# Two attentions over one x on one core: the first projection cut to 512 tokens, x's tiles loaded and turned in another order, the last products on the whole array

## The chip, the core and the metric

The kernel runs on one core of a Trainium2 chip. TensorE (PE) multiplies matrices into PSUM, VectorE (DVE) and ScalarE (ACT) read PSUM and work elementwise, GpSimd (POOL) works on SBUF only, and DMAs are issued from the queues of SP (SyncE), ScalarE and GpSimd. The metric is the device time of one execution in microseconds (us), the lower the better.

## The reference, cut to what matters

B = 1, S = 2048 tokens, D = 512, H = 32 heads of 16. Attention A has one k and v for all heads, attention B has its own per head. A gate mixes the two.

```python
x = A_x
g = sigmoid((x * gate_w).sum(-1, keepdims=True))
# A: q = x @ wq (32 heads), k = x @ wk and v = x @ wv (one head of 16)
# B: q, k, v = x @ wqkv, 32 heads each
# each: softmax(q k^T * 16 ** -0.5) v, heads joined, then @ wo
a = A(x, A_wq, A_wk, A_wv, A_wo)
b = B(x, B_wqkv, B_wo)
return g * a + (1 - g) * b
```

## The kernel before

**Numbers.** Every operand of a projection is split into two f16 parts, hi and lo (x by `x_split`, weights by `split_weight` on GpSimd, results by `split` on VectorE), and a product is three partial products, listed in `PARTS`. `by_tiles` (L189) does one partial product of 128x512 as eight matmuls of 64 rows and 32 columns of the array. The row halves go into two banks, which VectorE adds afterwards (`added`, L193 and L194, or the two adds of L450).

**Head.** The 16 tiles of x (128 tokens each, 256 KB) are loaded into `acc` by SP (L212). Each is turned by four transposes (`x_turn`, L264) and split: hi by ScalarE (L268), lo by VectorE (L269), into `xT`. `x_pair` does two tiles in one PSUM tile `pt`, `x_one` one tile in one bank of `aux`. Before the first exp the program turns tiles 0 to 7, projects the first 1024 tokens to the queries of A's first eight heads (192 matmuls in two units of 96), makes k and v of tiles 0 to 3 (`kv_products`, L297, 48 matmuls) and turns k (`k_turned`, L318, into `kA`), then turns tiles 8 to 11. Queries are laid out for the scores by 32 small DMAs (`lay`, L338): four tiles Q of two heads each (p = 0 to 3), each by eight pieces. The table `first` deals the pieces over the queues of SP, ScalarE and GpSimd.

**Exps.** The work is 2048 blocks u of two banks of 128 keys x 512 queries. Per block: `scores(u)` (L529, eight matmuls into one of two PSUM tiles `sc`), one exp on ScalarE (L533, 128x1024, into `pr`), and half a unit of `values` (L548, 16 matmuls, or eight pairs over two banks, two or more blocks later). One group is eight heads of A or B, in order a, b, a, b, ...: 256 blocks. Blocks 0 to 31 are p = 0 and 1 with the first 512 queries, 32 to 63 p = 2 and 3, and from block 64 on the second 512 queries are used. Block u uses key tile (u // 2) % 16, so k of tiles 4 to 7 is used from block 8 on, of 8 to 11 from 16, of 12 to 15 from 24.

**What lies between.** Each loop turn issues the scores, then what the table `early` has for this block, then values, then projection steps of eight matmuls, as many as a planner, `_Tasks`, thinks fit beside an exp (`EXP = 916`, `SCORES = 213`, `HALF = 428`, `PRODUCT = 216`, ns). Units have a block from which they may start and one at which they are due. `late()` adds up what is due; if it says so, an odd block gets one step more than fits. A unit of 12 steps starts only if its two banks (the pair of `aux` that the values don't use) stay free for it, that is not close before the pair changes, each 32 blocks. `add_side` queues work for VectorE, `move` queues `lay` calls, one per six blocks. Engines run their instructions in this program order.

**Tail.** After the last values, `emptied` adds the two banks (`raw`), DMAs sums and denominators apart (`oT`, `dT`), and `norm_pieces` gives per tile of 128 tokens `over` (reciprocal, L462) and `parts` (scaling L469, hi by ScalarE L470 and lo by GpSimd L471 for the last four tiles). `o_unit` multiplies with wo (three partial products, 24 matmuls), adds both banks into `acc` (L450, twice) and stores the tile (L452). What is left when the blocks are done is issued by `flush`.

## Time and profile before

| | us |
|---|---|
| median of 3 runs | 1957.51 |
| lowest, highest | 1956.01, 1959.62 |
| the profiled execution | 1959.14 |
| its span, first to last instruction | 1956.9 |
| ScalarE busy in the span | 1895.2 (97%) |
| TensorE busy | 1857.9 (95%) |
| VectorE busy | 756.9 (39%) |
| GpSimd busy | 444.7 (23%) |

The span is what the trace shows; the execution's time has 2.2 us more around it. A busy TensorE is not TensorE at its peak, since its matmuls overlap. The mean granted clock of TensorE over the span is 0.991 of full speed.

### The profile page before, as it was taken

The page shows a single profiled execution, that of the slowest core. Times are in us where ns is not written, and L with a number is a line of the kernel's source. Part 1 is how long each engine was busy: PE and PEld are TensorE (multiplying, and loading weights), DVE is VectorE, ACT ScalarE, POOL GpSimd, SP SyncE. Part 2 cuts the span into 40 slices and gives each one's busy share as a digit, 9 for nine tenths or more (in the row PEclk, how much of TensorE's full clock was granted, in tenths as well). Part 3 has the DMA queues.
Part 4 walks back from the last instruction along what each step waited for, and adds up shares of the span by engine and source line. Part 5 has one row for each costly group of instructions (what it writes and reads, how often), then busy time and mean ns, then how long its engine had stood idle before and what let it go on. Part 6 is the DMA issues. An engine that isn't in the chain of part 4 may idle for free.

```text
span 1956.9 us, 127404 instructions
## 1 busy us (share of the span) xinstructions
PE 1857.9 (95%) x59664; PEld 1060.7 (54%) x59664; DVE 756.9 (39%) x1429; ACT 1895.2 (97%) x2071; POOL 444.7 (23%) x840
## 2 busy tenths in 40 slices
PE   7999999999999999999999999999999999999995
PEld 4555655454555655555455655555455555555442
DVE  5344434343233344424234334443324334443432
ACT  4999999999999999999999999999999999999994
POOL 5344033230054031223034203302303502030000
PEclk8999999999999999999999999999999999999997
DMA  4121011110022010111012101100101201011101
GB/s 143 25 55 36 10 37 34 33 34 15 11 55 49 12 34 19 29 36 33 13 35 42 39 15 31 37 21 25 36 14 32 58 15 25 21 36 31 36 25 42
DMA packets 55736, 65.01 MB, mean 33 GB/s; under 512 B 21440, under 2 KB 29632, under 8 KB 55200
## 3 DMA queue, kind: packets, MB, share of 16 engines
q0 software_dynamic: 24112, 24.89, 6.4%
q1 hardware_dynamic: 30400, 31.46, 6.2%
q8 instruction: 469, 7.68, 1.7%
q14 instruction: 67, 0.55, 0.1%
q10 hardware_dynamic: 688, 0.43, 0.1%
HBM read 10.55 MB, written 4.19 MB: 8 GB/s over the span
## 4 chain that ended last, share of the span: by engine, by line
ACT 83%; issue 8%; PE 7%; DVE 2%; DMA 0%; SPq 0%; POOL 0%; ACTq 0%; DVEq 0%
ACT pr L533 82%; PE aux L548 3%; PE sc L529 2%; PE aux L189 2%; DVE xT L269 0%; DVE acc L450 0%; DMA acc<-in_A_x_dram 0%; PE aux L416 0%; ACT xT L268 0%; DVE dTb L462 0%; PE pt L264 0%; PE aux L297 0%; DMA dTb<-rawb 0%; PE aux L318 0%; PE aux L264 0%
## 5 line engine op out<-in xcount | busy, mean ns | idle before, releaser
L533 ACT ACTIVATE pr<-sc 128x1024 f32<-128x1024 f32 x2048 | 1884.6, 1191 | 12.6 <-PE sc L529 11.7
L548 PE MATMUL aux<-pr,vA 64*32 64x256 f32 x16384 | 685.3, 377 | 2.3 <-issue 1.9
L548 PE MATMUL aux<-pr,vB 64*32 64x256 f32 x16384 | 646.7, 376 | 0.1
L529 PE MATMUL sc<-Qa,kA 64*32 64x512 f16 x8192 | 453.4, 384 | 18.4 <-issue 0.3
L529 PE MATMUL sc<-Qb,K 64*32 64x512 f16 x8192 | 424.1, 385 | 41.8
L529 PEld LDWEIGHTS <-K 64*32 64x32 f16 x8192 | 209.3, 89 | 387.5 <-issue 309.0
L548 PEld LDWEIGHTS aux<-pr,vA 64*32 64x32 f32 x16384 | 335.7, 105 | 58.0 <-issue 15.1
L529 PEld LDWEIGHTS <-kA 64*32 64x32 f16 x8192 | 209.7, 90 | 277.3 <-issue 207.3
L548 PEld LDWEIGHTS aux<-pr,vB 64*32 64x32 f32 x16384 | 309.7, 105 | 35.4 <-issue 0.7
L450 DVE SCALAR_TENSOR_TENSOR acc<-aux,gate_up,acc 128x512 f32<-128x512 f32 x240 | 180.2, 751 | 326.6 <-PE aux L189 312.9
L338 POOL DMA_DIRECT2D Qa<-hia x118 | 57.8, 489 | 449.4 <-PE sc L529 299.1
L338 POOL DMA_DIRECT2D Qb<-hib x128 | 62.3, 486 | 359.5 <-DVE hib L201 181.7
L189 PE MATMUL aux<-w16ob,o16b 64*32 64x512 f16 x1536 | 80.3, 391 | 15.1 <-ACT o16b L470 13.2
L189 PE MATMUL aux<-xT,w16vb 64*32 64x512 f16 x1536 | 93.8, 376 | 0.1
L193 DVE TENSOR_SCALAR rawb<-aux 128x512 f32<-128x512 f32 x32 | 22.1, 689 | 179.9 <-PE aux L548 179.7
L338 POOL DMA_DIRECT2D K<-hik x128 | 61.5, 485 | 109.3 <-DVE hik L201 102.4
L189 PE MATMUL aux<-xT,w16kb 64*32 64x512 f16 x1536 | 82.2, 376 | 0.0
L189 PE MATMUL aux<-xT,w16qb 64*32 64x512 f16 x1536 | 79.9, 376 | 0.0
L189 PE MATMUL aux<-xT,w16qa 64*32 64x512 f16 x1536 | 79.5, 376 | 0.4 <-DVE xT L269 0.2
L189 PE MATMUL aux<-w16oa,o16a 64*32 64x512 f16 x1536 | 79.3, 376 | 0.0
L462 DVE RECIPROCAL dTa<-dTa 128x128 f32<-128x128 f32 x64 | 55.6, 918 | 59.8 <-DMA dTa<-rawa 59.8
L462 DVE RECIPROCAL dTb<-dTb 128x128 f32<-128x128 f32 x64 | 55.4, 916 | 52.9 <-DMA dTb<-rawb 52.9
(135 smaller groups left out, 991.2 us busy)
## 6 DMA issues: line engine op xcount, KB each, us to landing
acc<-in_A_x_dram SPq DMA_DIRECT2D x16, 256.0 KB, 5.9
dTa<-rawa SPq DMA_DIRECT2D x128, 32.0 KB, 2.6
oTa<-rawa SPq DMA_DIRECT2D x128, 32.0 KB, 3.2
K<-hik POOLq DMA_DIRECT2D x128, 32.0 KB, 2.7
K<-lok POOLq DMA_DIRECT2D x128, 32.0 KB, 2.9
Qb<-hib POOLq DMA_DIRECT2D x128, 32.0 KB, 2.5
Qb<-lob POOLq DMA_DIRECT2D x128, 32.0 KB, 2.8
out_dram<-acc SPq DMA_DIRECT2D x16, 256.0 KB, 2.6
```

The lines of the kernel that those rows point to most:

```text
L189: nc.tensor.matmul(out[n : n + COLS], lhsT[r, n : n + COLS], rhs[r], start=start, stop=stop)
L193: nc.vector.tensor_scalar(dst, outs[0], scale, None, op0=ALU.mult)
L338: queues[(8 * p + n) % len(queues)].dma_start(op[to : to + DH].rearrange("d (a q) -> d a q", a=2), state[part][rows])
L450: nc.vector.scalar_tensor_tensor(acc[:, t], bank, g, acc[:, t], op0=ALU.mult, op1=ALU.add)
L462: nc.vector.reciprocal(d, d)
L529: nc.tensor.matmul(sc[a : a + COLS, i], k[r, c * P + a : c * P + a + COLS], Q[src, gi, half, p][r, j * BLK : (j + 1) * BLK], start=True, s ...
L533: nc.scalar.activation(probs[u][:, :m], sc[:, :m], AF.Exp, scale=SCALE / (UP * UP))
L548: nc.tensor.matmul(o[32 * i : 32 * i + 32, cols], v[r], probs[at // ACT][r, at % ACT, cols], start=c == half == 0, stop=c == NT - 1 and ha ...
```

## The change

**Loads.** The q weights of the first group are asked for first and the o weights behind the three small loads of k, v and gate weights; x's tiles 0 to 3 stand ahead of both in the code. **Head.** Before the first exp only tiles 0 to 7 are turned, tiles 0 to 3 are projected (96 matmuls), and tiles 4 to 7 are turned behind the k and v of tiles 0 to 3. The second 512 tokens are a unit for the planner (from block 24, due at 40). `lay` moves half tiles, the first half over three queues, the second half by GpSimd. **Between exps.** `early` has one function per block: pieces of k and v (12 matmuls each), turns, and x's tiles 8 to 15, whose hi part is VectorE's too. **Tail.** For the last four tiles reciprocal and scaling alternate per tile, all of them are issued before the products, and `o_last` replaces `o_unit`: three matmuls over the whole array into one bank, one add, stores from SP and ScalarE by turns.

```diff
     def flush(self):
-        ahead = 0
         while self.open or self.units or self.side:
-            if self.side and ahead < 6 and not (self.units and ahead > 2):
+            while self.side and not self.open:
                 self.side.popleft()[1]()
-                ahead += 1
-                continue
-            ahead -= 3
...
-    first_w = load_w("a", 0, (nc.scalar, nc.gpsimd))
+    for t in range(4):
+        load_x(t, nc.sync)
+    first_w = load_w("a", 0, (nc.scalar, nc.gpsimd), ("q",))
     nc.scalar.activation(warm, warm, AF.Exp)
-    for t in range(NT):
+    for t in range(4, NT):
         load_x(t, nc.sync)
...
+    first_w += load_w("a", 0, (nc.scalar, nc.gpsimd), ("o",))
...
-        nc.scalar.activation(xT[:, 0, :, at], pt, AF.Copy, scale=UP)
+        if t < 8:
+            nc.scalar.activation(xT[:, 0, :, at], pt, AF.Copy, scale=UP)
+        else:
+            nc.vector.tensor_scalar(xT[:, 0, :, at], pt, UP, None, op0=ALU.mult)
...
+                        (nc.gpsimd if i else queues[(8 * p + n) % len(queues)]).dma_start(
+                            op[to : to + DH, i * BLK : (i + 1) * BLK], state[part][rows, i])
...
-            if i:
+            if late is not None:
+                todo.move([lambda p=p: lay(p, i) for p in range(4)])
+            elif i:
                 todo.move([lambda p=p: lay(p) for p in range(4)])
...
+    def o_last(src, gi, t, o16):
+        w, i = weights[src, gi, "o"], "ab".index(src)
+        bank = aux[t // 2 % 2][t % 2]
+        for n, (a, b) in enumerate(PARTS):
+            nc.tensor.matmul(bank, o16[:, a], w[:, b], start=n == 0, stop=n == 2)
+        nc.vector.scalar_tensor_tensor(acc[:, t], bank, gate_up[:, i, t : t + 1], acc[:, t], op0=ALU.mult, op1=ALU.add)
+        (nc.sync, nc.scalar)[t % 2].dma_start(out[t * P : (t + 1) * P, :], acc[:, t])
...
+            if ends:
+                todo.add([[lambda: o_last(src, gi, 8 * half + t8, o16)]], todo.now, todo.now)
+                return
...
-    x_pair(0)
+    for t in range(4):
+        x_one(t, aux[t // 2][t % 2])
     first_w[0]()
-    x_pair(2)
-    split_weight(wkv16[:, 0], wkv16[:, 1], wkv)
+    split(wkv16[:, 0], wkv16[:, 1], wkv)
+    nc.gpsimd.tensor_scalar(wkv, wkv, UP, None, op0=ALU.mult)
     first_w[1]()
-    for t in range(4, 8):
-        x_one(t, aux[t // 2 % 2][t % 2])
     late = []
-    first = (nc.sync, nc.scalar, nc.gpsimd, nc.sync) * 2 + (nc.sync, nc.gpsimd, nc.sync) * 8
+    first = (nc.sync, nc.gpsimd, nc.scalar, nc.sync, nc.gpsimd, nc.scalar, nc.sync, nc.gpsimd)
     turn[0] = 1
-    for unit in q_units("a", 0, 0, first, late):
-        for f in unit:
-            f()
-        turn[0] ^= 1
+    q_first, q_second = q_units("a", 0, 0, first, late)
+    for f in q_first:
+        f()
     while todo.moves:
         todo.moves.popleft()()
+    todo.add([q_second], 24, 40, 2200)
     for i in range(4):
-        kv_products(0, i, aux[0][0])
-    k_turned(0, aux[0][1])
-    x_pair(8)
-    x_one(10, aux[1][0])
-    x_one(11, aux[1][1])
+        kv_products(0, i, aux[1][0])
+    for t in range(4, 6):
+        x_one(t, aux[0][t % 2])
+    k_turned(0, aux[1][1])
+    for t in range(6, 8):
+        x_one(t, aux[0][t % 2])
...
-    early = {0: p1, 2: t1, 4: x_unit(12), 6: x_unit(13), 8: x_unit(14), 10: p2, 12: t2, 14: x_unit(15), 16: p3, 20: t3}
+    early = []
+    for b in range(1, 4):
+        if b > 1:
+            early += [x_unit(t)[0] for t in range(4 * b, 4 * b + 4)]
+        early += [f for unit in kv_units(b) for f in unit]
+    early = {u: [f] for u, f in enumerate(early)}
...
-            todo.add_side(over, todo.now + (4 if last and half else 10), [950])
-            todo.add_side(parts, todo.now + (4 if last and half else 13), [800])
+            if ends:
+                todo.add_side([f for both in zip(over, parts) for f in both], todo.now + 4, [950, 800])
+                return
+            todo.add_side(over, todo.now + 10, [950])
+            todo.add_side(parts, todo.now + 13, [800])
...
-            todo.add(q_units(src, gi, 1, pool), now if n else 21, start(n, 1) - 24, 2200)
+            todo.add(q_units(src, gi, 1, pool), now if n else 24, start(n, 1) - 24, 2200)
```

In the rows below, which come from the built programs and have no time in them, a name's number is its buffer, and the line numbers of the changed program are its own.

On ScalarE's queue ahead of the first exp (`pr<-sc`), before: the split of tile 7, two pieces of Q, and the splits of tiles 8 to 11.

```order
L268 ACTIVATE xT<-aux_85 128x4x128
L338 DMA Qa_399<-loa_194 16x1024 x2
L268 ACTIVATE xT<-pt_500 128x4x128 x2
L268 ACTIVATE xT<-aux_84 128x4x128
L268 ACTIVATE xT<-aux_85 128x4x128
L533 ACTIVATE pr_550<-sc_541 128x1024
```

Now, where four more pieces of Q stand right ahead of these:

```order
L339 DMA Qa_289<-hia_167 16x512
L339 DMA Qa_289<-loa_168 16x512
L339 DMA Qa_298<-hia_167 16x512
L339 DMA Qa_298<-loa_168 16x512
L270 ACTIVATE xT<-aux_82 128x4x128
L270 ACTIVATE xT<-aux_83 128x4x128
L270 ACTIVATE xT<-aux_82 128x4x128
L270 ACTIVATE xT<-aux_83 128x4x128
L553 ACTIVATE pr_420<-sc_411 128x1024
```

Eight issues of Q's pieces now stand ahead of the splits of tiles 4 to 7, and these ahead of the first exp; tiles 8 to 11 are gone from this place.

On VectorE after the first k turn between exps (`kA`), before: lo parts of x's tiles 12 to 14 and two maxima of weights (`stats`).

```order
L319 COPY kA<-aux_83 128x512
L269 SCALAR_TENSOR_TENSOR xT<-aux_82,xT 128x4x128
L198 TENSOR_REDUCE stats<-wqa_104 128x1
L198 TENSOR_REDUCE stats<-woa_107 128x1
L269 SCALAR_TENSOR_TENSOR xT<-aux_83,xT 128x4x128
L269 SCALAR_TENSOR_TENSOR xT<-aux_82,xT 128x4x128
```

Now, at the same place:

```order
L316 COPY kA<-aux_83 128x512
L194 TENSOR_REDUCE stats<-wqa_108 128x1
L272 TENSOR_SCALAR xT<-aux_82 128x4x128
L273 SCALAR_TENSOR_TENSOR xT<-aux_82,xT 128x4x128
L194 TENSOR_REDUCE stats<-woa_127 128x1
L272 TENSOR_SCALAR xT<-aux_83 128x4x128
L273 SCALAR_TENSOR_TENSOR xT<-aux_83,xT 128x4x128
L272 TENSOR_SCALAR xT<-aux_82 128x4x128
L273 SCALAR_TENSOR_TENSOR xT<-aux_82,xT 128x4x128
L272 TENSOR_SCALAR xT<-aux_83 128x4x128
L273 SCALAR_TENSOR_TENSOR xT<-aux_83,xT 128x4x128
```

Four tiles, 8 to 11, stand there with two instructions each, where three tiles had one each.

On VectorE in the tail, behind the last `raw`, before:

```order
L462 RECIPROCAL dTb_52040<-dTb_52040 128x128 x4
L469 SCALAR_TENSOR_TENSOR oTb_52039<-oTb_52039,dTb_52040 128x128
L450 SCALAR_TENSOR_TENSOR acc<-aux_84,gate_up,acc 128x512
L450 SCALAR_TENSOR_TENSOR acc<-aux_85,gate_up,acc 128x512
L469 SCALAR_TENSOR_TENSOR oTb_52039<-oTb_52039,dTb_52040 128x128
L450 SCALAR_TENSOR_TENSOR acc<-aux_84,gate_up,acc 128x512
L450 SCALAR_TENSOR_TENSOR acc<-aux_85,gate_up,acc 128x512
L469 SCALAR_TENSOR_TENSOR oTb_52039<-oTb_52039,dTb_52040 128x128 x2
L450 SCALAR_TENSOR_TENSOR acc<-aux_84,gate_up,acc 128x512
L450 SCALAR_TENSOR_TENSOR acc<-aux_85,gate_up,acc 128x512
L450 SCALAR_TENSOR_TENSOR acc<-aux_84,gate_up,acc 128x512
L450 SCALAR_TENSOR_TENSOR acc<-aux_85,gate_up,acc 128x512
```

Now:

```order
L475 RECIPROCAL dTb_52069<-dTb_52069 128x128
L482 SCALAR_TENSOR_TENSOR oTb_52068<-oTb_52068,dTb_52069 128x128
L475 RECIPROCAL dTb_52069<-dTb_52069 128x128
L482 SCALAR_TENSOR_TENSOR oTb_52068<-oTb_52068,dTb_52069 128x128
L475 RECIPROCAL dTb_52069<-dTb_52069 128x128
L482 SCALAR_TENSOR_TENSOR oTb_52068<-oTb_52068,dTb_52069 128x128
L475 RECIPROCAL dTb_52069<-dTb_52069 128x128
L482 SCALAR_TENSOR_TENSOR oTb_52068<-oTb_52068,dTb_52069 128x128
L444 SCALAR_TENSOR_TENSOR acc<-aux_82,gate_up,acc 128x512
L444 SCALAR_TENSOR_TENSOR acc<-aux_83,gate_up,acc 128x512
L444 SCALAR_TENSOR_TENSOR acc<-aux_84,gate_up,acc 128x512
L444 SCALAR_TENSOR_TENSOR acc<-aux_85,gate_up,acc 128x512
```

Reciprocals and scalings now stand ahead of all adds, the reciprocals one per scaling, and each tile has one add from a bank of its own in place of two from a shared pair.

## Rows read from the trace of the kernel before

**Rows 1.** The page's chain that ended last: shares of the span by line.

```profile
ACT pr L533 82%; PE aux L548 3%; PE sc L529 2%; PE aux L189 2%; DVE xT L269 0%; DVE acc L450 0%; DMA acc<-in_A_x_dram 0%; PE aux L416 0%; ACT xT L268 0%; DVE dTb L462 0%; PE pt L264 0%; PE aux L297 0%; DMA dTb<-rawb 0%; PE aux L318 0%; PE aux L264 0%
```

**Rows 2.** The chain near the end: start us, length us, engine and line.

```profile
1914.03 0.87 ACT pr L533
...
1925.95 1.25 ACT pr L533
```

**Rows 3.** Timeline, head: start us, busy us, engine, line, operation, out<-in, count, idle before.

```profile
7.69 1.12 PE L264 MATMUL pt<-ident,acc 128*128 128x128 f32 x4 [0.24 <-DMA acc<-in_A_x_dram]
...
8.43 1.15 POOL L207 TENSOR_TENSOR w16qa<-wqa,w16qa 128x512 f16<-128x512 f32 x1
...
10.19 0.60 ACT L268 ACTIVATE xT<-pt 128x512 f16<-128x512 f32 x1 [0.76 <-DVE xT L269]
...
10.82 0.69 DVE L269 SCALAR_TENSOR_TENSOR xT<-pt,xT 128x512 f16<-128x512 f32 x1 [0.66 <-ACT xT L268]
...
21.82 1.42 ACTq L338 DMA_DIRECT2D Qa<-loa  x2
...
28.42 1.04 ACT L533 ACTIVATE pr<-sc 128x1024 f32<-128x1024 f32 x1
...
36.96 0.66 PE L264 MATMUL aux<-ident,acc 128*128 128x128 f32 x4
...
41.98 1.36 PE L297 MATMUL aux<-wkv,xT 128*128 128x33 f16 x48 [0.81 <-DVE xT L269]
```

**Rows 4.** Stretches: the exps alone: us, busy (count), clock, DMA share, GB/s.

```profile
28.00:60.00 32.00, 24.27 (x26) 0.94 0.18 48
```

**Rows 5.** The chain, head: start us, length us, engine, buffer and line.

```profile
12.76 2.85 PE aux L189 x95
...
18.74 0.61 DVE ya L193
...
30.68 0.13 DVE k L304
...
32.13 0.61 PE aux L318 x4
...
60.79 0.71 ACT pr L533
```

**Rows 6.** Timeline of the tail, columns as in Rows 3.

```profile
1933.13 3.39 DVE L462 RECIPROCAL dTb<-dTb 128x128 f32<-128x128 f32 x4 [3.27 <-DMA dTb<-rawb]
...
1936.43 0.23 DVE L469 SCALAR_TENSOR_TENSOR oTb<-oTb,dTb 128x128 f32<-128x128 f32 x1
...
1936.70 0.30 ACT L470 CAST o16b<-oTb 128x128 f16<-128x128 f32 x1 [9.50 <-DVE oTb L469]
...
1945.43 1.48 PE L189 MATMUL aux<-w16ob,o16b 64*32 64x512 f16 x24 [2.25 <-ACT o16b L470]
...
1946.98 1.62 DVE L450 SCALAR_TENSOR_TENSOR acc<-aux,gate_up,acc 128x512 f32<-128x512 f32 x2 [1.73 <-PE aux L189]
```

**Rows 7.** The chain's last piece on VectorE.

```profile
1951.04 0.75 DVE acc L450
```

**Rows 8.** Stretches, all engines, after the last values.

```profile
1933.20:1951.80 18.60, 6.71 (x96) 1.40 (x96) 10.07 (x16) 1.10 (x4) 1.65 (x4) 0.50 0.13 45
```

**Rows 9.** The page's DMA issues: queue, count, KB each, us to landing.

```profile
acc<-in_A_x_dram SPq DMA_DIRECT2D x16, 256.0 KB, 5.9
...
out_dram<-acc SPq DMA_DIRECT2D x16, 256.0 KB, 2.6
```

**Rows 10.** Timeline of TensorE in a stretch with doubled products.

```profile
615.46 0.63 PE L548 MATMUL aux<-pr,vA 64*32 64x256 f32 x16
...
615.89 0.63 PE L189 MATMUL aux<-xT,w16vb 64*32 64x512 f16 x16
...
617.83 0.63 PE L189 MATMUL aux<-xT,w16vb 64*32 64x512 f16 x16
```

**Rows 11.** The page's groups: one that GpSimd issues.

```profile
L338 POOL DMA_DIRECT2D Qa<-hia x118 | 57.8, 489 | 449.4 <-PE sc L529 299.1
```

More of the change, by code (lines that the diff above doesn't have):

```diff
@@ L215, in _fast, with load_w @@
     todo = _Tasks()
-    def load_w(src, gi, queues=(nc.sync, nc.sync)):
+    def load_w(src, gi, queues=(nc.sync, nc.sync), which=("q", "k", "v", "o")):
         cols = slice(gi * P, (gi + 1) * P)
@@ L222, in one @@
         def one(part, at, bufs):
+            if part not in which:
+                return
             w = inp.tile([P, BLK], F32, tag="in", name=f"w{part}{src}{gi}")
@@ L267, in x_split @@
         at = slice(t * P, (t + 1) * P)
-        nc.scalar.activation(xT[:, 0, :, at], pt, AF.Copy, scale=UP)
+        if t < 8:
+            nc.scalar.activation(xT[:, 0, :, at], pt, AF.Copy, scale=UP)
+        else:
+            nc.vector.tensor_scalar(xT[:, 0, :, at], pt, UP, None, op0=ALU.mult)
         nc.vector.scalar_tensor_tensor(xT[:, 1, :, at], pt, UP, xT[:, 0, :, at], op0=ALU.mult, op1=ALU.subtract)
-    def x_pair(t2):
-        pt = ps_s.tile([P, 2, NK, P], F32, tag="sc", name=f"pt{t2}")
-        for i in range(2):
-            x_turn(t2 + i, pt[:, i])
-        for i in range(2):
-            x_split(t2 + i, pt[:, i])
     def x_one(t, bank):
@@ L330, in project, with lay @@
         state = {}
-        def lay(p):
+        def lay(p, i=None):
             op, n = put(p), 0
@@ L337, in lay @@
                     to = hh * 64 + n % 4 * DH
-                    queues[(8 * p + n) % len(queues)].dma_start(
-                        op[to : to + DH].rearrange("d (a q) -> d a q", a=2), state[part][rows])
+                    if i is None:
+                        queues[(8 * p + n) % len(queues)].dma_start(
+                            op[to : to + DH].rearrange("d (a q) -> d a q", a=2), state[part][rows])
+                    else:
+                        (nc.gpsimd if i else queues[(8 * p + n) % len(queues)]).dma_start(
+                            op[to : to + DH, i * BLK : (i + 1) * BLK], state[part][rows, i])
                     n += 1
@@ L357, in product @@
             split(state["hi"][:, i], state["lo"][:, i], y)
-            if i:
+            if late is not None:
+                todo.move([lambda p=p: lay(p, i) for p in range(4)])
+            elif i:
                 todo.move([lambda p=p: lay(p) for p in range(4)])
-            if late is None:
+            if late is None or i:
                 absmax(kind, n0 + i, y)
@@ L375, in put @@
         def put(p):
-            Q[src, gi, half, p] = ops.tile([P, 2 * BLK], F16, tag="Q", name=f"Q{src}{gi}{half}{p}", bufs=8)
+            if (src, gi, half, p) not in Q:
+                Q[src, gi, half, p] = ops.tile([P, 2 * BLK], F16, tag="Q", name=f"Q{src}{gi}{half}{p}", bufs=8)
             return Q[src, gi, half, p]
@@ L573, in emptied @@
             over, parts = zip(*[norm_pieces(src, gi, half, t8, last) for t8 in range(4 * j, 4 * j + 4)])
-            todo.add_side(over, todo.now + (4 if last and half else 10), [950])
-            todo.add_side(parts, todo.now + (4 if last and half else 13), [800])
+            if ends:
+                todo.add_side([f for both in zip(over, parts) for f in both], todo.now + 4, [950, 800])
+                return
+            todo.add_side(over, todo.now + 10, [950])
+            todo.add_side(parts, todo.now + 13, [800])
     def flag_stats():
```

1 line of the change is left out of this document (removed).

## The prediction

> **What bounds the kernel now.** I read the page first, then the head and the tail in the timeline and the chain, then stretches. Of the chain that ends last, 82% of a span of 1956.9 us is ScalarE's exps [rows 1]. So an edit counts only if it starts the first exp sooner, spares ScalarE a gap between exps, or shortens what follows the last one. The last 14 exps begin at 1914.03 and the last of them at 1925.95 [rows 2], so the pace is 11.92/13 = 0.917. 2048 exps at that pace are 1878 us. The first starts at 28.42 [rows 3], the last ends at 1914.03 + 13.16 = 1927.2, and 29.7 us follow. These sum to 1936: some 21 us are lost between exps. The first 26 exps lose most: they begin before 60 us [rows 4], the 27th at 60.79 [rows 5], so 32.37 us went by where 26 x 0.917 = 23.8 would do, a loss of 8.5. (I count exps as blocks from 0, each with two 512-column score banks.)
>
> **The tail.** Before, VectorE runs four reciprocals from 1933.13, then per tile a scaling, and behind it two bank adds; the next tile's scaling stands behind them [rows 6], so each tile pays the whole round of VectorE, ScalarE, TensorE and VectorE again. The last add starts at 1951.04 [rows 7] and ends at 1951.8; 5.1 us of store and closing follow. In the changed order four pairs of reciprocal and scaling come first, then four adds, one per tile. Reciprocals step by (1936.43 - 1933.13)/4 = 0.825, a scaling takes 0.23: four pairs end at 1933.13 + 4 x 1.055 = 1937.35. The first tiles' products lie beside the later pairs. The fourth scaling starts at 1937.12; ScalarE's copy 0.27 later, at 1937.39 (as 1936.43 to 1936.70); 0.30 for the copy and 0.04 to hand over put its products at 1937.73, with GpSimd's subtraction beside the first two of them; and the sum is ready 1.55 later (1945.43 to 1946.98), at 1939.3 [rows 6]. Three whole-array products move the same 3 x 512 columns as 24 products of which eight share the array, so I take the same 1.55; the row holds at the clock of 0.50 that this stretch was granted [rows 8], after TensorE had idled. The first three adds of 0.75 run 1937.35 to 1939.6, the fourth ends at 1940.35. That is 11.4 us earlier. The stores went out one per round and now all go within 2.5 us: a lone store lands in 2.6 us, sixteen crowded loads of the same size in 5.9 [rows 9]. Four are nearer to the lone case: I take 0.4 off, **11.0 gained**, between 8.1 and 11.4.
>
> **The head.** On SP the first instruction is still x's tile 0 and on ScalarE still the q weights; what moves is the o weights, behind three small loads on GpSimd. Tile 3's transposes began at 7.69 [rows 3], after four x tiles and two weights of 256 KB each: with one of the six out of the way at most a sixth of those 7 us is saved, and nothing if the contest is only shifted. I take 7.3. (The Trainium skill, DMA: Bandwidth & Descriptors, Issuing engines are not separate DMA queues, says that transfers of all issuers share the same 16 DMA engines and interleave; by it x gains only from bytes that are taken away, not from its place in the code. No row here tells the two apart; with nothing saved the sum would be 0.4 less.) Then four transposes 1.12, ScalarE's split 0.60, VectorE's 0.69: 9.8 with the hand-overs. The q weights are split by 8.43 + 1.15 = 9.58, as before. Now 96 products. As many took 2.85 before (12.76 to 15.61 [rows 5]); 24 took 1.48 at a clock of 0.50 [rows 6, 8], so 96 would take up to 5.9. Tile 3's four transposes took 1.12 against 0.66 later [rows 3]: TensorE starts slow, and now only 16 transposes, with gaps, lead in. I take 4.7, ending at 14.5. VectorE's five steps, 3.13 (15.61 to 18.74 [rows 5]), give hi at 16.95 and lo at 17.65. Here the change adds a wait: eight DMA issues on ScalarE, where two took 1.42 [rows 3], stand ahead of the splits of tiles 4 to 7 and so of all exps. The second needs lo, so they end at 17.65 + 7 x 0.71 = 22.6. Then tiles 4 and 5 are split; tile 6 needs tile 4's bank back: 22.6 + 0.60 + 0.69 + 0.05 = 23.95; two tiles' transposes at 1.12, ScalarE 0.60: the first exp at 26.9, **1.5 gained**. With a fast TensorE throughout (2.85; 0.66 twice) and tile 3 at 7.0 it is 23.8, with 5.9 and 7.7 it is 28.5. The k/v weight split on VectorE lies in the idle time under those products; of the pieces of p = 0 and 1, GpSimd and SP issue six each, from 17.65 on: at 0.49 to 0.7 and with 2.6 to land [rows 9, 11] they are there by 24.5.
>
> **The first 24 blocks** now carry eight x tiles, twelve k/v pieces and three k turns. A plain block costs TensorE 0.43 for values (615.46 to 615.89). Two blocks with 24 products took 1.94 (to 617.83 from 615.89): less two values 1.08 is left for three groups of eight products and two of scores, each eight instructions that share the array: 0.216 each [rows 10]. So scores and values are 0.64. An x tile adds 0.59 (0.66 less the overlap with the next, an estimate) [rows 3]: 1.23, or 0.31 over the pace, 2.5 for eight. A k/v piece is a fourth of 1.36 [rows 3]: 0.98, 0.07 over, for nine of them with values 0.6. Each turn waits in TensorE's order for VectorE's chain from 30.68 to 32.13, 1.45, after the last piece, then takes its own 0.4 (0.61 at 32.13 [rows 5], less at speed), 0.43 for values and 0.22 for the next scores: 2.5, of which the two exps that ScalarE has in hand cover 1.83. That is 0.7 for the first turn; I estimate 0.9 for the second, when less is in hand, and 1.6 for the third, behind three weight maxima on VectorE. VectorE works 1.4 per x tile, more than a block's length, which holds the fourth tile back by another 0.9. Sum 7.2, plus 0.8 for blocks run before TensorE is fast again: 8.0 against 8.5, **0.5 gained**. Bounds: TensorE's own excess alone, 3.1; with slow products up to block 8, 11.
>
> **Crowding afterwards.** The second 512 tokens' projection and what is due behind it now wait until block 37. The planner then counts itself late and puts 16 products (two steps of eight) into odd blocks: by the order of its instructions 26 times before block 128 where it was none, and 27 against 18 times up to block 350; from there on the two orders agree until block 2004. Such a pair of blocks lasts the 1.94 of [rows 10] where two exps need 1.83: 0.11 each, 35 x 0.11 = 3.8; the first pair of a burst is partly covered by TensorE's lead of one score tile, so I take **3.3 lost** (1.5 to 6). The 32 extra DMA issues on GpSimd at 0.49 [rows 11] from block 44 on cost nothing as long as block 64 finds its pieces (the third rival prices that).
>
> **Sum.** 11.0 + 1.5 + 0.5 - 3.3 = 9.7. The profiled execution took 1959.14 us, 2.2 around its span; it would take 1949.4. The median of the three runs is 1957.51, 1.6 lower: **1947.8**.
>
> **Rivals.** *The crowding costs double*: an in-order TensorE that waits for VectorE in the first blocks (11 lost there, not 8.0) and again under the bursts (6, not 3.3). For it: VectorE's work in the first 24 blocks, eight tiles at 1.4 plus chains and maxima, fills nearly all of their 22 us. Against it: afterwards it has time. Gain 4.0: 1953.5. *TensorE fast from the first product*: the first exp at 23.8 and no slow blocks: gain 9.7 + 3.1 + 0.8 = 13.6, 1943.9. Against it: the doubled duration of the first transposes. (The Trainium skill, TensorE: Matmul & The Clock Gate, What's actually happening, has half rate as the resting state, released by activity; the 0.50 of [rows 8] after idling agrees, and by it this rival is unlikely.) *Slower*: the second half of Q arrives late for block 64. Its products end with block 44, at 26.9 + 8.0 + 44 x 0.917 = 75.2; VectorE 3.1; GpSimd then issues eight pieces for p = 0 and eight for p = 1, 16 x 0.49 = 7.8, from 78.3 to 86.1, and landing takes some 2.6 [rows 9, 11]: 89. Block 64 begins at 93.6. Only if it came 5 us later would block 64 wait, and from 15 us on the whole gain is gone. Against it: on GpSimd's queue only four weights' splits stand ahead, twelve steps like the 1.15 of [rows 3], handed to it from block 12 on. *The stores crowd as the loads did*: 3 less, 1950.7. *Nothing happens at the head*: 1.5 less, 1949.3, in the main case's range.
>
> **Chances.** As summed, 1944.5 to 1951.2: 0.66, the crowded stores with it. Crowding doubled 0.15, fast from the start 0.13, slower 0.03, others 0.03. The range from 1942.5 to 1953.5 leaves out the ends of both middle rivals. A measurement of this kernel tells 0.2%, 3.9 us, from nothing, so faster means under 1953.6: 0.66 + 0.13 + two thirds of 0.15 = 0.89; same 0.07; slower 0.04.
>
> **What would show it.** Right: the last add ends 13 us after the last exp, not 24.6; eight issues on ScalarE's queue before the first exp, which starts near 27; the 27th exp near 59; exps at 1.02 in odd blocks between 37 and 125. Wrong: a first exp after 28.5, a landing of the last store over 5 us, an exp near block 64 that waits for Q, or a stall over 2 us at a k turn.

## The result, and the profile after

The changed kernel takes 1961.15 us (median of 20 runs, 1957.41 to 1964.83), the kernel before 1956.43 (20 runs): a ratio of 1.0021 [1.0014, 1.0028], taken over all runs of both. 1947.8 was forecast. The profiled execution spans 1959.7 us where before spanned 1956.9, so 2.8 us are to be found in the two traces. The medians differ by 4.7 us: the profiled execution of before was one of its slower ones (1959.14), and the rest is in no trace.

The share of the exps in the chain fell from 82% [rows 1] to 79%, and links appear in it that were not there, GpSimd's issues of Qb and the landing of Qb. The page's chain by line:

```profile
ACT pr L553 79%; PE aux L568 3%; PE sc L549 2%; PE aux L185 1%; DMA acc<-in_A_x_dram 1%; PE aux L265 0%; POOL Qb L336 0%; PE aux L294 0%; DMA Qa<-hia 0%; PE aux L443 0%; DMA Qb<-lob 0%; DVE dTb L475 0%; DMA dTb<-rawb 0%; POOL K L336 0%; DMA K<-hik 0%
```

The ledger is made by counting exps. The view of one line's instructions gives for a window their count and the first and last start; what exceeds 0.9166 us for each step, the pace of the last exps in both traces, is lost. The loss is a net one, since plain blocks step by as little as 0.90. Of after, in four windows (at the head, to 275 us, around block 256, the rest):

```profile
L553 ACT ACTIVATE pr<-sc x31: 1018/1024/1098, 25.4 to 65.5; 128x1024 f32<-128x1024 f32 x31
```
```profile
L553 ACT ACTIVATE pr<-sc x220: 1017/1046/1243, 65.5 to 274.2; 128x1024 f32<-128x1024 f32 x110
```
```profile
L553 ACT ACTIVATE pr<-sc x35: 1018/1098/1245, 274.2 to 309.6; 128x1024 f32<-128x1024 f32 x35
```
```profile
L553 ACT ACTIVATE pr<-sc x1765: 1018/1239/1247, 309.6 to 1935.0; 128x1024 f32<-128x1024 f32 x197
```

The first says 40.1 us for 30 steps, 12.6 lost. Counted alike in both traces:

| stretch | before | after | difference | forecast |
|---|---|---|---|---|
| first exp starts at | 28.42 | 25.44 | -3.0 | -1.5 |
| lost, to 66 us | 8.6 | 12.6 | +4.0 | -0.5 |
| lost, 66 to 275 us | 4.0 | 8.0 | +4.0 | +3.3 |
| lost, 275 to 310 us | 0.1 | 4.2 | +4.2 | not priced |
| lost, 310 us to the last exp | 8.7 | 8.5 | -0.2 | 0 |
| last exp's start to the end of the span | 30.9 | 24.7 | -6.2 | -11.0 |
| sum | | | +2.8 | -9.7 |

The ledger is that of one execution of each kernel. The long stretch behind 310 us is not steady: in the changed kernel and its variants it lost from 8.5 to 16.9 us.

**Head.** The timeline, columns as in [rows 3], answers to that group:

```profile
7.64 0.66 PE L265 MATMUL aux<-ident,acc 128*128 128x128 f32 x4 [0.23 <-DMA acc<-in_A_x_dram]
...
9.63 2.57 PE L185 MATMUL aux<-xT,w16qa 64*32 64x512 f16 x88 [0.23 <-POOL w16qa L203]
...
15.24 0.60 ACTq L339 DMA_DIRECT2D Qa<-hia  x1
...
21.47 1.08 ACT L270 ACTIVATE xT<-aux 128x512 f16<-128x512 f32 x2 [12.53 <-DMA Qa<-hia]
...
22.84 1.97 PE L265 MATMUL aux<-ident,acc 128*128 128x128 f32 x8 [4.94 <-DVE xT L273]
...
25.44 1.02 ACT L553 ACTIVATE pr<-sc 128x1024 f32<-128x1024 f32 x1
```

Tile 3 is turned at 7.64 in 0.66 us, and the projection ends at 9.63 + 2.57 = 12.2. The two turns that come last took 1.97. The windows of these stretches (us, busy us and count of PE, PEld, DVE, ACT and POOL, clock, DMA share, GB/s), the tail's last with them, show the granted clock: 1.00 (2.4 GHz) at the projection, 0.50 (1.2 GHz) where TensorE had idled before.

```profile
8.99:12.20 3.21, 2.98 (x99) 1.42 (x99) 1.20 (x3) 0.00 (x0) 2.27 (x3) 1.00 1.04 394
22.80:24.90 2.10, 2.06 (x16) 1.69 (x16) 1.19 (x3) 0.65 (x2) 0.00 (x0) 0.50 0.14 31
1947.40:1953.00 5.60, 4.45 (x10) 1.34 (x10) 2.97 (x4) 0.00 (x0) 1.50 (x4) 0.50 0.33 121
```

**First blocks.** Block 4, which turns the second group's keys, with VectorE's operations on them and GpSimd's splits of the next group's weights beside them; then one block with a tile of x:

```profile
28.79 0.61 POOL L202 CAST w16kb<-wkb 128x512 f16<-128x512 f32 x1
...
29.02 0.43 DVE L304 TENSOR_SCALAR k<-k 128x64 f32<-128x64 f32 x1
...
29.48 1.20 POOL L203 TENSOR_TENSOR w16kb<-wkb,w16kb 128x512 f16<-128x512 f32 x1
29.71 1.06 DVE L198 SCALAR_TENSOR_TENSOR kn<-k,kn 128x64 f16<-128x64 f32 x1
...
31.74 0.61 PE L315 MATMUL aux<-ident,kn 128*128 128x128 f16 x4 [2.29 <-DVE kn L308]
```
```profile
48.17 1.02 ACT L553 ACTIVATE pr<-sc 128x1024 f32<-128x1024 f32 x1 [0.37 <-PE sc L549]
...
48.56 0.66 PE L568 MATMUL aux<-pr,vA 64*32 64x256 f32 x16
...
49.02 0.42 PE L549 MATMUL sc<-Qa,kA 64*32 64x512 f16 x8
...
49.37 0.66 PE L265 MATMUL aux<-ident,acc 128*128 128x128 f32 x4
...
49.56 1.02 ACT L553 ACTIVATE pr<-sc 128x1024 f32<-128x1024 f32 x1 [0.37 <-PE sc L549]
...
49.95 0.66 PE L568 MATMUL aux<-pr,vA 64*32 64x256 f32 x16
```

VectorE's two operations end at 29.45 and 30.77, 0.05 and 0.09 us behind GpSimd's. In a block with a tile TensorE goes from values (48.56) to scores (49.02), to the tile (49.37) and to the next values (49.95): 0.46, 0.35 and 0.58, in all 1.39, as the exps' starts do.

**Block 256**, the first of the second group: GpSimd issues its first query piece, and TensorE's scores wait:

```profile
274.40 0.48 POOL L336 DMA_DIRECT2D Qb<-hib  x1 [78.60 <-PE sc L549]
...
284.42 0.61 PE L549 MATMUL sc<-Qb,K 64*32 64x512 f16 x4 [2.47 <-DMA Qb<-lob]
```

Before, the same first piece:

```profile
263.61 0.56 POOL L338 DMA_DIRECT2D Qb<-hib  x1 [96.39 <-DVE hib L201]
```

Blocks 256 and 257 use sixteen pieces. The sixteenth left at 281.57 and landed at 284.29, 0.13 us ahead of the scores that waited; before, it landed at 273.52, and block 257 began its scores at 276.01.

**Tail**, answering to [rows 6] and [rows 7]:

```profile
1942.18 0.95 DVE L475 RECIPROCAL dTb<-dTb 128x128 f32<-128x128 f32 x1 [3.31 <-DMA dTb<-rawb]
...
1943.37 0.94 DVE L475 RECIPROCAL dTb<-dTb 128x128 f32<-128x128 f32 x1
1943.49 0.30 ACT L483 CAST o16b<-oTb 128x128 f16<-128x128 f32 x1 [7.29 <-DVE oTb L482]
...
1947.06 0.30 ACT L483 CAST o16b<-oTb 128x128 f16<-128x128 f32 x1 [0.89 <-DVE oTb L482]
1947.32 1.57 POOL L484 TENSOR_TENSOR o16b<-oTb,o16b 128x128 f16<-128x128 f32 x4 [6.96 <-issue]
...
1947.80 4.45 PE L443 MATMUL aux<-w16ob,o16b 128*128 128x512 f16 x10 [2.92 <-POOL o16b L484]
...
1948.44 0.75 DVE L444 SCALAR_TENSOR_TENSOR acc<-aux,gate_up,acc 128x512 f32<-128x512 f32 x1 [1.42 <-PE aux L443]
...
1952.28 0.75 DVE L444 SCALAR_TENSOR_TENSOR acc<-aux,gate_up,acc 128x512 f32<-128x512 f32 x1 [0.53 <-PE aux L443]
```

The first copy is there at 1943.79, yet GpSimd's four subtractions begin at 1947.32, behind 6.96 us in which they wait for nothing shown. Ten of the twelve products follow, at a granted clock of 0.50, one tile per 1.28 us.

### The profile page after: what moved, and what is told of

Same layout as the page of the kernel before. It is cut to its first block, busy times and chain, and to the rows that moved or that the text cites. A ratio compares the mean times of both kernels' runs of the same rounds, so it can differ in the third digit from the quotient of the medians.

```text
span 1959.7 us, 127274 instructions
## 1 busy us (share of the span) xinstructions
PE 1856.4 (95%) x59580; PEld 1056.1 (54%) x59580; DVE 761.1 (39%) x1435; ACT 1896.8 (97%) x2063; POOL 460.9 (24%) x872
## 3 DMA queue, kind: packets, MB, share of 16 engines
q10 hardware_dynamic: 1168, 1.02, 0.2%
## 4 chain that ended last, share of the span: by engine, by line
ACT 79%; issue 10%; PE 7%; DMA 1%; POOL 1%; DVE 1%; SPq 0%; ACTq 0%; DVEq 0%; POOLq 0%
ACT pr L553 79%; PE aux L568 3%; PE sc L549 2%; PE aux L185 1%; DMA acc<-in_A_x_dram 1%; PE aux L265 0%; POOL Qb L336 0%; PE aux L294 0%; DMA Qa<-hia 0%; PE aux L443 0%; DMA Qb<-lob 0%; DVE dTb L475 0%; DMA dTb<-rawb 0%; POOL K L336 0%; DMA K<-hik 0%
## 5 line engine op out<-in xcount | busy, mean ns | idle before, releaser
L553 ACT ACTIVATE pr<-sc 128x1024 f32<-128x1024 f32 x2048 | 1889.4, 1165 | 21.3 <-PE sc L549 19.8
L568 PE MATMUL aux<-pr,vA 64*32 64x256 f32 x16384 | 668.2, 377 | 1.4 <-issue 1.1
L549 PE MATMUL sc<-Qb,K 64*32 64x512 f16 x8192 | 428.9, 385 | 44.6 <-DMA Qb<-lob 2.9
L549 PE MATMUL sc<-Qa,kA 64*32 64x512 f16 x8192 | 444.1, 384 | 22.9 <-issue 1.6
L549 PEld LDWEIGHTS <-kA 64*32 64x32 f16 x8192 | 205.0, 90 | 286.8 <-issue 212.4
L568 PEld LDWEIGHTS aux<-pr,vA 64*32 64x32 f32 x16384 | 321.6, 105 | 53.6 <-issue 9.1
L463 DVE SCALAR_TENSOR_TENSOR acc<-aux,gate_up,acc 128x512 f32<-128x512 f32 x232 | 174.3, 751 | 324.2 <-PE aux L185 310.9
L185 PE MATMUL aux<-xT,w16vb 64*32 64x512 f16 x1536 | 81.3, 376 | 0.1
L185 PE MATMUL aux<-xT,w16kb 64*32 64x512 f16 x1536 | 77.3, 376 | 0.0
L185 PE MATMUL aux<-w16ob,o16b 64*32 64x512 f16 x1440 | 73.9, 376 | 0.0
```

The lines of the kernel that those rows point to most:

```text
L185: nc.tensor.matmul(out[n : n + COLS], lhsT[r, n : n + COLS], rhs[r], start=start, stop=stop)
L463: nc.vector.scalar_tensor_tensor(acc[:, t], bank, g, acc[:, t], op0=ALU.mult, op1=ALU.add)
L549: nc.tensor.matmul(sc[a : a + COLS, i], k[r, c * P + a : c * P + a + COLS], Q[src, gi, half, p][r, j * BLK : (j + 1) * BLK], start=True, s ...
L553: nc.scalar.activation(probs[u][:, :m], sc[:, :m], AF.Exp, scale=SCALE / (UP * UP))
L568: nc.tensor.matmul(o[32 * i : 32 * i + 32, cols], v[r], probs[at // ACT][r, at % ACT, cols], start=c == half == 0, stop=c == NT - 1 and ha ...
```

## The experiments

They ran on three chips, on which the kernel before took 1959.9 to 1962.3 us; each ratio is against runs of before on the same chip at the same time. The unaltered changed kernel was not run there, so its 1.0021 comes from another set of runs.

### The tail

**The new tail alone**: before with the changed flush, `o_last`, `norm_pieces` and `emptied`, nothing else.

> The kernel before with only the new tail (reciprocals and scalings by turns, GpSimd's four subtractions, three products of the whole array into one bank each, one add a tile, stores by SP and ScalarE). Theory A, from the trace of after: GpSimd's subtractions start only when VectorE has run its last scaling, so the four products of the lower part come after that, one tile per 1.28 us; the stretch from the last exp's start to the span's end falls from 29.7 to about 23.5 us and the time falls by about 6.2 us, 0.997 of before. Theory B, the prediction's own: the subtractions run beside the products, 11.0 us are saved (0.9944), and what after lost was lost elsewhere.

0.9962 [0.9949, 0.9975]: theory A in size, though its cause falls further down. From the last exp's start to the end it is 24.3 us, and the first subtraction comes 12.5 us after the last exp's start. The tail gains 7 us and not 11; what the changed kernel lost beyond that, it lost elsewhere.

**VectorE subtracts**, each behind the next tile's reciprocal:

```diff
-            (nc.gpsimd if ends else nc.vector).tensor_sub(o16[:, 1], o, o16[:, 0])
+            if ends:
+                return
+            nc.vector.tensor_sub(o16[:, 1], o, o16[:, 0])
...
+        def rest():
+            nc.vector.tensor_sub(o16[:, 1], o, o16[:, 0])
```

> As the run with the new tail alone, but the four subtractions are VectorE's, each issued behind the next tile's reciprocal (0.29 us each by the row of before). Theory A (GpSimd is held while VectorE works): the first product of a lower part starts about 3 us sooner, TensorE's twelve products of 0.43 us spread over the time of the reciprocals, and the last add ends about 14 us after the last exp's start in place of 16.8: some 3 us under the run with GpSimd's subtractions, 9 under before (0.9953). Theory B (the products at the slow clock, 1.28 us a tile, set the end whoever subtracts): at most 1 us under it, since the four subtractions add 1.2 us to VectorE's own chain.

0.9977 [0.9966, 0.9988], a miss. The tail did get 2.3 us shorter, but the first exp came at 34.3 in place of 28.8. Timeline of GpSimd, start:

```profile
0.73 0.20 POOL masks.py:197 MEMSET ident<- 128x128 f32 x1 [0.29 <-POOLq L825]
9.97 0.28 POOL masks.py:199 TENSOR_SCALAR_AFFINE_SELECT ident<-ident 128x128 f32<-128x128 f32 x1 [9.04 <-issue]
```

**The same with one plain GpSimd operation behind its reduction:**

```diff
         nc.gpsimd.partition_all_reduce(top, part, P, ReduceOp.max)
+        nc.gpsimd.tensor_sub(part, part, part)
```

> The kernel before with the new tail and VectorE's subtractions (as the run with them alone), and one small GpSimd subtraction right behind its reduction over the partitions, late in the last group. In that run GpSimd's second instruction, the mask of the identity, started at 9.97 us in place of 1.23, and the first exp at 34.27 in place of 28.86, while the stretch from the last exp to the end was 22.0 us in place of 24.3. Theory A: the reduction leaves GpSimd set up for it, and where no plain operation follows it the next execution begins with some 9 us of setting up; the small subtraction takes that off the start, the first exp is back at 28.9 and the time is 2.3 us under the run with the new tail alone, 0.995 of before. Theory B: that start was chance or belongs to VectorE's subtractions; then the first exp stays near 34 and the time at 0.9977.

0.9941 [0.9927, 0.9955]: theory A. The first exp is back near 28.7, and the set-up (this text's word for that idle time) is now seen by itself, between reduction and subtraction:

```profile
1875.19 0.39 POOL L610 PARTITION_ALL_REDUCE top<-part  x1 [130.84 <-DVE part L609]
1882.64 0.20 POOL L611 TENSOR_TENSOR part<-part 128x16 f32<-128x16 f32 x1 [7.05 <-DMA oTb<-rawb]
```

The DMA named in the second row had landed at 1881.48, 1.2 us earlier, and the subtraction doesn't read what it brought; in the nine kernels with this line the time is 6.8 to 7.2 us.

**A gap on VectorE**, GpSimd subtracting, to learn who holds the subtractions:

```diff
+                first = lambda: o_last(src, gi, 8 * half + 4, o16s[src, gi, half][:, :, 4 * P : 5 * P])
+                fns = [f for both in zip(over, parts) for f in both]
+                todo.add_side(fns[:4] + [first] + fns[4:], todo.now + 4, [950, 800])
```

> The kernel before with the new tail and GpSimd's subtractions, but VectorE's first add is issued behind the second scaling, so that VectorE must stand still there until the first tile's three products are done. Theory A (GpSimd's subtraction is held while VectorE runs reciprocals and scalings): the first subtraction starts within 0.4 to 1.3 us of the end of the second scaling, about 10 us after the last exp's start, in place of 12.5. Theory B (GpSimd needs some 3.5 us from the first copy on whatever VectorE does, to start its first such operation): it starts at about 12.4 as before, and VectorE stands still until then.

1953.83 us in its one run. VectorE's second scaling ended at 1935.38 and VectorE stood still from there, yet:

```profile
1930.70 0.48 POOL L579 DMA_DIRECT2D oTb<-rawb  x1
...
1935.09 0.29 DVE L474 SCALAR_TENSOR_TENSOR oTb<-oTb,dTb 128x128 f32<-128x128 f32 x1
...
1938.77 0.81 POOL L476 TENSOR_TENSOR o16b<-oTb,o16b 128x128 f16<-128x128 f32 x2 [7.59 <-issue]
```

Theory A falls. B's "3.5 us from the first copy" is not it either, since here it is 4.5: what stays much the same is the idle time behind GpSimd's last issue, 7.59 here, 6.96 in the changed kernel, and 6.98 in before, where the reciprocals hid it:

```profile
1938.34 0.42 POOL L471 TENSOR_TENSOR o16b<-oTb,o16b 128x128 f16<-128x128 f32 x1 [6.98 <-issue]
```

**The new tail with the set-up moved ahead**, the one added line of above and nothing else, on before and on the changed kernel:

> The kernel before with the new tail as the change has it (GpSimd subtracts) and one small GpSimd subtraction right behind its reduction over the partitions, some 50 us before the end. Theory A (the first plain operation behind that reduction costs GpSimd 7 us of setting up, which in the tail began only behind its last issue): the set-up is over when the tail begins, the first subtraction starts about 9.2 us after the last exp's start in place of 12.5, each runs beside the next tile's reciprocal, and the last add ends about 14.7 in place of 18.2 after the last exp's start: the tail of the prediction, 3.5 us under the run with the new tail alone (0.9962), about 0.9944. Theory B (VectorE's work holds the subtractions): they start at 12.4 as before, 0.996.

> The changed kernel with nothing but the small GpSimd subtraction added behind the reduction. Theory A: its tail becomes the forecast one, the stretch from the last exp's start to the end falls from 24.7 to about 21 us, and the time from 1.0021 to about 1.0003 of before. Theory B: no change, 1.002.

On before 0.9950 [0.9934, 0.9966], 1948.50 us; on the changed kernel 1.0012 [1.0001, 1.0023]. Tail of the first:

```profile
1936.51 0.30 ACT L475 CAST o16b<-oTb 128x128 f16<-128x128 f32 x1 [7.21 <-DVE oTb L474]
...
1936.89 0.42 POOL L476 TENSOR_TENSOR o16b<-oTb,o16b 128x128 f16<-128x128 f32 x1 [3.42 <-ACT o16b L475]
...
1939.96 2.72 DVE L436 SCALAR_TENSOR_TENSOR acc<-aux,gate_up,acc 128x512 f32<-128x512 f32 x4
...
1940.45 0.43 POOL L476 TENSOR_TENSOR o16b<-oTb,o16b 128x128 f16<-128x128 f32 x1 [0.77 <-ACT o16b L475]
```

Each subtraction starts 0.08 us after its copy, and the last add ends at 1942.68, 14.6 us after the last exp's start. The span of the changed kernel with it ends 21.6 us after the last exp's start, where the unaltered one had 24.7. The traces carry this, not the times: 0.9950 and the 0.9962 of the new tail alone aren't separated by their intervals, nor are 1.0012 and 1.0021.

### Head and middle

**The mended tail (VectorE's) on the changed kernel.**

> The changed kernel with the same tail (VectorE's subtractions, and the small GpSimd subtraction behind the reduction). If the tail is worth the same on either start and middle: 2.5 us under the changed kernel, 1.0008 of before; and against the kernel before with the same tail (0.995 expected) some 11 us more, which is then what start and middle of the change cost together. If start and middle cost nothing and the tail alone failed: level with that kernel.

1.0008 [0.9999, 1.0017], against 0.9941 for before with the same tail: start and middle of the change cost 13 us on this chip (medians 1964.73 and 1951.77).

**The first b group's queries due sooner:**

```diff
-        due = start(n + 1, 0) - 36
+        due = start(n + 1, 0) - (36 if n else 52)
```

> The changed kernel with one number of the planner altered: the products of the first b group's queries are due 16 blocks sooner. They then end near block 236 in place of 245, by the order on TensorE; as many odd blocks are doubled as in the changed kernel. Theory A: the 4.36 us between exps 256 and 257 are a wait for the last pieces of those queries, since their products end later than before and 32 pieces then take GpSimd 0.49 us each; the gap falls to about 1 us and the time by 3 to 4 us (0.998 to 0.9985 of after, level with before). Theory B: GpSimd's own backlog of issues is what is late; then the pieces still leave near 274 us and nothing is gained.

1.0007 [0.9996, 1.0017]: theory A, level with before. The pieces leave from 267.69 on, and the wait is gone (34.8 us for 38 steps, nothing lost):

```profile
L553 ACT ACTIVATE pr<-sc x39: 1021/1099/1249, 274.8 to 309.6; 128x1024 f32<-128x1024 f32 x39
```

**The weights' splits held back**, then also VectorE's reductions over them:

```diff
+                if (src, gi, part) == ("b", 0, "k"):
+                    nc.gpsimd.tensor_copy(held, kA[0:1, S - 1 : S])
-            todo.add_side(load_w(*groups[1]), now + 12, [0])
+            todo.add_side(load_w(*groups[1]), now + 24, [0])
```

> The changed kernel, with GpSimd's splits of the second group's weights held back until the last keys of the first group are turned (one copy of one element in front of them, which reads the last column of those keys); TensorE's order is the same. Theory A: beside GpSimd's splits VectorE's short operations on the first keys take 3.0 us in place of 1.45, and the gap behind block 4 is 4.36 us for that; it falls to about 2.8, the first 28 blocks lose about 11 in place of 12.6, and the time falls by 1.5 to 2 us. Theory B: the gap is the order's own (TensorE turns the keys in the block right behind their products, and waits for VectorE's nine operations whatever GpSimd does); it falls by under 0.5 us and the time stays.

1.0033 [1.0020, 1.0046], slower: the first 28 blocks lost 10.1 us, but VectorE's reductions now stood behind GpSimd's splits, the gates' sigmoid behind them, and on ScalarE the exps stood behind its step of that sigmoid, which waited 3.40 us for VectorE:

```profile
69.19 0.21 ACT L143 ACTIVATE z<-z 128x16 f32<-128x16 f32 x1 [3.40 <-DVE z L142]
```

So the reductions were moved as well:

```diff
-                todo.add_side([lambda: absmax(f"w{part}_{src}", gi, w)], todo.now + 4, [560])
+                todo.add_side([lambda: absmax(f"w{part}_{src}", gi, w)], todo.now + (24 if (src, gi) == ("b", 0) else 4), [560])
```

> As the run with the weights' splits held back, but VectorE's reductions over those weights are issued 20 blocks later as well. There the gap behind block 4 fell from 4.36 to 1.93 us and the first 28 blocks lost 10.1 in place of 12.6, but blocks 28 to 64 lost 6.2 in place of 0.6, 4.65 of it at block 33. Theory A: VectorE stood behind those reductions, which wait for GpSimd's splits; issued later they wait for nothing, blocks 28 to 64 lose about 1, and the time is 2 us under the changed kernel, 1.001 of before. Theory B: the loss at block 33 has another cause and stays: 1.003.

1.0003 [0.9992, 1.0013]: theory A. The two VectorE operations of above take 0.18 and 0.23 us, the keys are turned at 29.84, and to 66 us 9.4 are lost (39.7 us for 33 steps), where three changed kernels on these chips with the splits in their place lost 11.3 to 12.9:

```profile
28.63 0.18 DVE L307 TENSOR_SCALAR k<-k 128x64 f32<-128x64 f32 x1
...
29.08 0.23 DVE L198 SCALAR_TENSOR_TENSOR kn<-k,kn 128x64 f16<-128x64 f32 x1
...
29.84 0.40 PE L318 MATMUL aux<-ident,kn 128*128 128x128 f16 x4 [0.78 <-DVE kn L311]
```
```profile
L556 ACT ACTIVATE pr<-sc x34: 1018/1023/1128, 25.4 to 65.1; 128x1024 f32<-128x1024 f32 x34
```

**A tile between products and turn:** `early += kv + xs[:1] + turned + xs[1:]`.

> The changed kernel with one tile of x between the products and the turn of the keys, for the second and third group of keys. Theory A: TensorE stands 2.3 to 2.8 us behind VectorE's nine operations on the keys because the turn is in the block right behind their products; a block of 1.4 us between them hides as much of it at each of the two, the gap behind block 4 falls from 4.36 to about 3, and the time by 2 us, to 1.001 of before. Theory B: the tile's own turn waits for a bank that the same operations of VectorE set free, and its split stands behind them: the gaps move to the next block, and the time falls by under 0.5 us.

1.0013 [1.0002, 1.0025]: unclear. Block 4 fell to 1.39 us, but blocks 5 and 6 took 2.45 and 2.63, TensorE waiting for VectorE 1.19 and 1.17: at the first turn mostly theory B. The second turn was hidden (block 13 took 1.40 in place of 1.98), and 10.4 were lost to 66 us.

**All of these together.**

> The changed kernel with each cost that was found taken out: the mended tail (as in the run of the changed kernel with it, 1.0008 of before), the weights' splits held back, a tile of x between products and turn of the keys, and the first b group's queries due 16 blocks sooner. If the costs found are those that matter: about 3.0 us less for the first 28 blocks, 1 for the turns, 3.3 for block 256: 0.997 of before, 5 to 6 us above the kernel before with the same tail (0.994); what stays is TensorE's own work of the blocks with tiles and keys and the doubled blocks. If they only move elsewhere: 0.9995 or above.

0.9982 [0.9973, 0.9992], 1956.93 us, between the two expectations: the costs found are costs, and taking them out together beats before, but not before with the mended tail.

**Edits at before's head**, with the splits held back: two turns of keys later, and in the second and fourth run x's tiles 8 to 11 behind the first exp; with VectorE's tail, then with GpSimd's. The diff is that of the first and third. In the last two expectations "the same tail", "the first run of these" and "the run before it" mean before with the new tail and the set-up moved ahead.

```diff
-    early = {0: p1, 2: t1, 4: x_unit(12), 6: x_unit(13), 8: x_unit(14), 10: p2, 12: t2, 14: x_unit(15), 16: p3, 20: t3}
+    early = {0: p1, 4: x_unit(12), 5: t1, 6: x_unit(13), 8: x_unit(14), 10: p2, 12: x_unit(15), 14: t2, 16: p3, 20: t3}
```

> The kernel before with the tail of the fastest run so far (VectorE's subtractions, GpSimd's small one behind the reduction), the second group's weight splits held back until the first group's keys are turned, and two of the turns of keys two or three blocks later (first to block 5, second to block 14). In the run with that tail alone the blocks 2, 10, 12, 16 and 21 took 2.71, 2.37, 1.76, 1.60 and 2.18 us, and the first 28 lost 7.9. Theory A: blocks 2 and 12 are TensorE's wait for VectorE's nine operations, hidden by the distance, and GpSimd's splits beside blocks 7 to 18 lengthen VectorE's work; the first 28 lose about 5.5 and the time falls by 2 us, to 0.993. Theory B: what VectorE and TensorE have to do in these blocks sets the pace whatever the order; the gaps move and the time stays at 0.994.

> As the run before it, and the tiles 8 to 11 of x are turned in blocks behind the first exp as well, with VectorE making the upper part of tiles 8 to 15. ScalarE's four splits of 0.6 us, between 25.9 and 28.8 us, then no longer stand ahead of the first exp, which comes at about 26.4 in place of 28.7; each of the four blocks that takes a tile lasts 1.39 in place of 0.92, so 1.9 us are given back. Theory A: 0.5 us gained against the run before it. Theory B: VectorE, with 1.4 us a tile and the keys' operations, is what blocks 2 to 15 then wait for, and they lose 2 us or more on top.

> The kernel before with the same tail, weight splits held back and two turns of keys later, x's tiles where they were. In its profile with VectorE's subtractions the first 28 blocks lost 5.9 in place of 7.9 us: 2 us under the first run of these, 0.9934, if that is worth the time; level with it if the wait only moves.

> As the run before it, with the head of the run that turned x's tiles 8 to 11 behind the first exp (weight splits held back, turns of keys later). If the head's edits are worth what their profile showed, the first exp at 27.5 in place of 28.7 and 7.6 lost in the first 28 blocks in place of 7.9: 1.5 us under the run before it, 0.9936. If not: level with it.

0.9957 [0.9944, 0.9970], 0.9944 [0.9931, 0.9958], 0.9944 [0.9928, 0.9960] and 0.9957 [0.9944, 0.9970], with five or six runs each. The profiles show the head's gain (5.6 lost to 66 us in place of 8.4 in the third), but the times don't separate these from the two plain mended tails (0.9941, 0.9950): inconclusive. Before with the new tail and one added line, 0.9950, is the simplest of these versions, and none is shown to be faster.

## Why the prediction was wrong

Between the 9.7 us of gain forecast and the 2.8 lost in the traces lie 12.5: 4.8 in the tail, 4.5 in the first blocks, 4.2 at block 256 and 0.7 by crowding, less 1.5 at the head and 0.2 behind block 256.

**The tail: right in its design, wrong in one clause.** "With GpSimd's subtraction beside the first two of them" is the step that failed. With the set-up moved ahead it came true: the last add ended 13.4 us after the last exp's end, forecast 13.1, and the stretch from the last exp to the end is 21.3 us where before had 30.9, 9.6 gained. In the changed kernel it waited until 1947.32. The row that would have told it was there: 6.98 us of idling without a releaser at before's first subtraction. I read the durations in that stretch and not the idle times. A pair of reciprocal and scaling takes 1.19 us and not 1.055, since four reciprocals in a row overlapped (0.825 from one to the next, 0.94 alone) and alternating ones don't. The end came 6.7 us after the last add, in the changed kernel as in that run, where before it was 5.1: the stores and the closing cost 1.6 and not 0.4. 24.6 less 13.4 less 1.6 are the 9.6. The changed kernel with the added line, whose trace has all four landings, puts this on the stores:

```profile
out_dram<-acc SPq DMA_DIRECT2D x2, 256.0 KB, 3.1
out_dram<-acc ACTq DMA_DIRECT2D x2, 256.0 KB, 4.1
```

The last three took 3.9 to 4.2 us where [rows 9] has 2.6, and the span ended 2.66 us behind the last: part of what the rival of the crowded stores had.

**The head: more than forecast.** I had TensorE at 4.7 us for the 96 products; at a granted clock of 1.00 it took 3.2, from 8.99 to 12.2. The rest held (eight issues on ScalarE until 21.4, tiles 6 and 7 at 0.50). This was half of the rival with a fast TensorE: tile 3's turn and the projection ran at 1.00, the last two turns did not.

**The first blocks: wrong in sign.** Forecast 8.0 lost, 12.6 were. The steps that failed: "scores and values are 0.64" held for blocks in which every product shares the array, not beside whole-array products, where it is 0.81, so a tile's block took 1.39 and not 1.23; a block with a k/v piece took 1.21 and not 0.98. That is 1.3 for eight tiles and 1.8 for the eight pieces of the third and fourth group. For the tiles VectorE's two steps fill 1.38 of the same 1.39, and no run told the two apart; in the blocks with pieces TensorE goes from values to scores to piece to values without a wait (0.46, 0.35 and 0.40). And "each turn waits for VectorE's chain, 1.45": at the first turn it took 3.0, because GpSimd's splits had moved onto it. Block 4 took 4.36, so 3.4 were lost there and not 0.7; with the splits held back it took 1.9 to 2.0, about as long as the other two turns. Part of the loss is TensorE's clock, granted at 0.50 from 31.7 to 33.8, behind its wait of 2.29. The four loads stand behind the query pieces on SP. These left from 15.24 in place of 21.09, and were twelve half tiles in place of twenty, so the loads came 11 us sooner. The first split began at 27.24, before at 38.37:

```profile
38.37 1.49 POOL L205 TENSOR_SCALAR wkb<-wkb 128x512 f32<-128x512 f32 x1 [12.10 <-DMA wkb<-in_B_wqkv_dram]
```

I had put those splits behind block 12, where the planner places them; here the order of GpSimd's queue, not the planner, set when they ran. The two runs with the splits held back lost 10.0 and 9.5 to 66 us, 1.3 to 3.4 less than the three with the splits in their place. This is near what the first rival had for these blocks (11 lost, TensorE waiting for VectorE), though without GpSimd. The sign of being wrong came too, a stall over 2 us at a k turn.

**Crowding: right.** 4.0 more lost against 3.3, by 35 more doubled blocks (52 and 17 in the traces); twenty odd blocks from 37 to 117 took 1.02, as the sign said. On one of the three chips, with equal tails, 66 to 275 us lost 9.0 against 3.1, which the same 35 don't explain; part of it is single stalls of TensorE, one of 0.78 us amid the scores of block 160, which the profile lays to a DMA of other keys. They stay open.

**Not priced: block 256.** The rival asked whether the moved half would be late for block 64. It was not. Late was what stands last in the queue of products, the queries due at block 256: their pieces left from 274.40, before from 263.61, and before they had had 2.5 us to spare. That cost 4.2, and the run with the earlier due date took the wait away.

With equal tails on one chip the ledger adds up, which it does for any two traces, since it shares out one span: the changed kernel with the added line against before with it, +11.3 us of span, is -2.2 for the first exp, +2.9 to 66 us, +5.9 to 275, +3.6 at block 256, +0.8 after it, +0.3 in the tail.

## What to carry to other kernels

Read the idle time ahead of each engine's first instruction in a stretch, even where something longer hides it: shortening the cover turns it into the bound. Work that leaves the start of a kernel is not gone; follow it to the last deadline in the same queue, and look for what had little margin there. And when an engine's queue becomes shorter, ask what behind it now starts sooner and beside whom.

## What was not expected of the hardware

- GpSimd stood 6.79 to 7.59 us before its first plain operation after a reduction over the partitions, with no instruction shown. The Trainium skill (GPSIMD Engine Reference, Instruction dispatch) gives about 6 us for the first call to code that must be loaded, with nothing visible in a profile; the runs agree in kind, and measured more.
- The state seems to outlive the execution: in the one kernel where no plain operation follows the reduction, the identity's second step on GpSimd began at 9.97 us, behind 9.04 of idling, and at 1.23 in before; one plain operation behind the reduction took it away. That the execution before it left this behind is inferred, since a profile holds one execution.
- Beside GpSimd's splits VectorE's short operations between SBUF tiles took 1.06 and 0.43 us in place of 0.23 and 0.18, and ended within 0.1 us of GpSimd's instructions. The Trainium skill (SBUF — State Buffer, SBUF: two separate sides) has the two engines share a pair of ports that one holds for a whole instruction; these rows agree. A third one, 0.61 in place of 0.18, ended amid a GpSimd split, so the account isn't complete. The subtractions of the tail looked like the same and were not.
